# Attention, Fourier mixing and a two-layer MLP: a host layout without reversed copies, block 0 prepared inside the attention, and the blocks' loads spread

## The chip, the cores and the metric

One core of a Trainium2 chip. The time is the device time of one execution in microseconds (us). The engines are TensorE (PE; PEld is its weight load), VectorE (DVE), ScalarE (ACT), GpSimd (POOL) and SyncE (SP), which here only issues DMAs. A queue named SPq or POOLq is the sequencer that issues for that engine.

## The reference

```python
# q, k, v: (8, 8, 576, 64); per batch and head
out_d  = softmax(q_d k_d^T / 8) v_d     # q_d, k_d, v_d: means over 4 neighbours, 144 positions
out_lc = softmax(mask(q k^T / 8)) v     # mask: |i - j| < 4
x = repeat(out_d, 4) + out_lc           # as (8, 576, 512)
u = x + real(fft(fft(x, axis=1), axis=2))
un = (u - mean(u)) / sqrt(var(u) + 1e-6)
out = u + relu(un @ w_ch1) @ w_ch2      # 512 -> 2048 -> 512
```

## The kernel before

**Attention, some 330 us.** For each of 8 batches there are a pooled attention (`Pooled`, four pairs of heads), a local one (`Unit`, five spans of 128 positions, each with two windows of 64) and the Fourier part (`Mix`). `Unit.load` and `load_v` fetch `qkT` and `vaug` by SP; `sum_in` makes the pooled sums of four neighbours; `Pooled.sum_v` adds up four loads in `vsum` by accumulating DMAs of POOL. In the upper half of a batch the windows run backwards: `sum_in` writes reversed, and `Unit.copy_p` copies the transposed weights reversed and clears one column on POOL. `Mix` uses the symmetry in both axes: POOL adds a half of the columns to the other half, read reversed (`cross`), VectorE makes sum and difference (`fold`), ScalarE and POOL split into two parts (`split_high`, `split_low`), TensorE multiplies by waves (`sequence`, `mix`), and ScalarE copies the lower columns mirrored into the upper ones (`mirror`). Three results per batch go to DRAM: `ud` (pooled), `ul` (local) and `um` (mixed).

**Blocks, the rest.** 4608 tokens are 9 blocks of four tiles of 128. `Block.load` (693) brings a tile in three parts: part 0 copies `ul` in several pieces by SP (line 712), parts 1 and 2 add `um` (707) and `ud` (705) by accumulating DMAs of POOL. `stats`, `norm`, `turn` and `turn_high`/`turn_low` make the normed and transposed tile in two parts; `prepare` places them in the order. For each f of 16, `first` has 12 products (`hps`), `high` and `low` make the two parts of its relu, and `second` has 12 products into four sums (`acc`). `finish` adds and `store` writes out. Tiles and turned tiles are doubled: block n+1 uses the places of block n-1. The order is block 0 with f 0 to 4, block 1 with f 0 to 4, block 0 with f 5 to 15, then the rest of block 1 and blocks 2 to 8. The weights come as 64 quarters of 64-bit numbers; `Quarter` fetches each by SP and joins it on ACT, POOL and DVE (`size`, `clamp`, `join`, `high`, `low`). f 0 and 1 are decoded in the attention, the others behind it.

**The order.** Nothing is planned by cost. Every step is put in a list by `at(time, step)`; the times are numbers in the table `AT`, in units of which 20 are a batch (some 2 us each in the attention), and f takes 3.28 units. The steps are issued in the order of these numbers, each engine and queue runs its own in that order, and waits are put in where data or a place need it. `close_b` and `close_a` (838, 843) give places of the attention to the blocks: after `close_a` block 1 gets its tiles. Block 0's loads stand at units 120 to 160.5, its norms behind `close_b` (164.9), block 1's loads behind `close_a` (167.7). A later block's loads begin 6 units behind the start of the block ahead of it, its first norm at 12.

Of the kernel before, what the change touches and what calls it, by code (L numbers as in the profile page):

```python
# [22 lines left out]
    "pooled": (1.15, 0.05, -1.8, -2.74, -3.55),  # L23
    "mix": (18.82, 18.55, 17.92),
    "local_steps": (0, 1.66, 2.96, 4.76, 5.65, 7.95, 9.34),
    "pooled_steps": (0, 1.56, 3.05, 4.81, 5.63, 7.85, 9.33),
    "qk": (-12.1, 2.19),
    "sums": (-2.36, 0.44),
    "sum_v": (-12.96, -6.64, -4.76, 2.36),
    "load_v": (0.51,),  # L30
    "store_pooled": (0.1, 0.2),
    "crosses": ((1, 4.59), (2, 7.41), (0, 9.2)),
    "folds": ((3, 5.97), (1, 4.28), (2, 8.26), (0, 10.0)),
    "splits": (0.74, 0.9, 1.64),
    "z": (9.51, 12.03, 12.81, 15.82),
    "sequence": (12.92, 1.78, 0.82, 1.66),
    "mixed": (20.32, 2.6, 0.2, 0.9, 1.47, 2.03, 2.91),
    "store_local": (9.66,),
    "ffn": (3.75, 1.64),
    "decode": (49.49, 9.96, 8.98, 1.2, 1.74),  # L40
    "decode_steps": (-1.47, 0.24, 0.83, 2.1, 2.96),
    "first_norms": (0.57, 0.81, 2.43, 0.6),
    "second_norms": (0.03, 1.47, 0.8, 1.83),
    "add": (14.25, 2.77, 2.2),
# [6 lines left out]
TILES = 4  # L51
# [14 lines left out]
def kernel(  # L66
# [43 lines left out]
    um = [dram.tile([2, NSL * P, DM], F32, name=f"um{b}") for b in range(B)]  # L110
# [20 lines left out]
    unTs = {}  # L131
# [74 lines left out]
    maskb = p2.tile([P, W], BF16, name="maskb", bufs=1)  # L206
# [4 lines left out]
    nc.gpsimd.memset(odt[:, :, DM:], 0.0)  # L211
# [34 lines left out]
    class Pooled:  # L246
# [74 lines left out]
        def result(self, h0):  # L321
# [7 lines left out]
                out=odt[:GH, :, h0 * D : (h0 + 2) * D].rearrange("g t (h d) -> g t h d", h=2),  # L329
# [4 lines left out]
        def move(self):  # L334

            x = xab[self.b % 2]
            STORE.dma_start(out=odt[GH:GX, 0, :DM], in_=odt[W:GH, 1, :DM])
            STORE.dma_start(out=x[W:, NSL - 1, 0, :DM], in_=odt[:W, 1, :DM])

        def store(self):  # L340
            STORE.dma_start(out=ud[self.b].rearrange("(t g) c -> g t c", t=2), in_=odt[:GH, :, :DM])

        def plan(self):
            b = self.b
            stages = [self.scores, self.maxima, self.exps, self.transpose_p, self.copy_p, self.values, self.result]
            for r in range(4):
                at(pooled_at(b) + AT["sum_v"][r], self.sum_v, r)
# [10 lines left out]
    class Unit:  # L358
        def __init__(self, u):
            self.u, self.b, self.m = u, u // NPAIR, u % NPAIR  # L360
            self.s0 = SPANS[self.m]
            self.wins = [(st, st + W // 2 > HS) for st in STARTS[self.m]]

# [9 lines left out]
        def sum_in(self):  # L373

            if self.m == 0:
                sums[self.b] = pd.tile([P, 2, HP, G], F32, name="sums", bufs=1)
            g0 = self.s0 // 4
            lo = g0 if self.m == 0 else SPANS[self.m - 1] // 4 + P // 4
            hi = g0 + P // 4
            out = sums[self.b].rearrange("p i h g -> p (i h) g")  # L380
            x = self.qkT.rearrange("p i h (g r) -> p (i h) g r", r=4)
            for a, e in ((lo, min(hi, GH)), (max(lo, GH), hi)):
                if a < e:
                    to = out[:, :, a:e] if e <= GH else out[:, :, G + GH - 1 - a : G + GH - 1 - e : -1]
                    nc.vector.tensor_reduce(out=to, in_=x[:, :, a - g0 : e - g0], axis=AX.X, op=ALU.add)  # L385
# [51 lines left out]
        def copy_p(self):  # L437
            pT = self.pT = p2.tile([P, HP, 2, W], F32, name="pT", bufs=NUM_P)
            tpv = self.tp.rearrange("p (h n w) -> p h n w", h=HP, n=2)
            backs = [back for _, back in self.wins]  # L440
            if backs[0] == backs[1]:
                parts = [(slice(0, 2), backs[0])]
            else:
                parts = [(slice(n2, n2 + 1), back) for n2, back in enumerate(backs)]
            for r, back in parts:
                if back:

                    nc.gpsimd.memset(pT[:, :, r, 0:1], 0.0)
# [64 lines left out]
    class Mix:  # L513
# [8 lines left out]
        def cross(self, t):  # L522
            pq = self.pq[t] = psq.tile([P, 2, HD], F32, name="pq", bufs=3)
            xa, xb = (xab[self.b % 2][:, :, i] for i in range(2))
            for i, (u, v) in enumerate(((xa, xb), (xb, xa))):
                nc.gpsimd.tensor_tensor(out=pq[:, i], in0=u[:, t, 0:HD], in1=v[:, t, DM:HD:-1], op=ALU.add)


        def fold(self, t):
# [4 lines left out]
            else:  # L534
                a, b = odt[:, 0, 0:HD], odt[:, 0, DM:HD:-1]
# [511 lines left out]
```

## Time and profile before

| | us |
|---|---|
| median of 3 runs (lowest, highest) | 1204.2 (1194.73, 1205.47) |
| profiled execution, whole time | 1203.31 |
| its span, first to last instruction | 1201.5 |
| mean granted TensorE clock | 0.959 |
| TensorE, VectorE, ScalarE, GpSimd busy | 1108.2 (92%), 526.5 (44%), 366.0 (30%), 277.8 (23%) |

Each engine runs its own instructions in order, and busy time is the sum of their durations. "Idle before" is how long an engine stood before an instruction, and the name behind the arrow is what ended it. The granted clock is 1.00 at 2.4 GHz and 0.50 at 1.2 GHz. Only waits on the path to the end cost time.

### The profile page before, as it was taken

How to read it: one execution, taken by the hardware profiler on the slowest of the kernel's cores; microseconds unless marked ns; L12 is line 12 of the kernel's file. 1: busy time of each engine (PE TensorE's matmuls, PEld its weight loads, DVE VectorE, ACT ScalarE, POOL GpSimd, SP SyncE). 2: the span in 40 equal slices, each digit the busy share in tenths (PEclk: the TensorE clock that was granted, in tenths of full speed). 3: DMA queues.
4: the chain of work that ended last, by engine and by line, in shares of the span. 5: the costliest groups of instructions: out<-in, count | busy, mean ns of one | idle time of the engine just before them, and what ended most of it. 6: DMA issues, size and time to landing. Idle time of an engine off the chain costs nothing.

```text
span 1201.5 us, 20868 instructions
## 1 busy us (share of the span) xinstructions
PE 1108.2 (92%) x8304; PEld 927.0 (77%) x8304; DVE 526.5 (44%) x1218; ACT 366.0 (30%) x1102; POOL 277.8 (23%) x411
## 2 busy tenths in 40 slices
PE   4899889887868999999999999999999999899998
PEld 4788778776757888787788788788788788688887
DVE  3767777875678898222222221222222222122111
ACT  3667766784734444110110110111111111011010
POOL 2223432442484655203002001200200300200000
PEclk9788899997978999999999999999999999999999
DMA  9768667885684543605004103202301500500000
GB/s 293 196 182 261 207 176 217 287 238 140 160 229 121 143 124 97 140 1 127 14 1 109 31 1 96 44 1 75 66 1 50 91 1 36 106 1 1 35 1 35
DMA packets 59144, 124.12 MB, mean 103 GB/s; under 512 B 8024, under 2 KB 8152, under 8 KB 58792
## 3 DMA queue, kind: packets, MB, share of 16 engines
q1 hardware_dynamic: 45400, 93.25, 24.2%
q0 software_dynamic: 13648, 29.55, 14.2%
q8 instruction: 65, 1.06, 0.4%
q14 instruction: 31, 0.25, 0.1%
HBM read 89.89 MB, written 31.75 MB: 101 GB/s over the span
## 4 chain that ended last, share of the span: by engine, by line
PE 55%; DMA 8%; SPq 4%; DVE 3%; issue 1%; POOL 1%; ACT 0%; POOLq 0%; DVEq 0%; ACTq 0%
PE hps L767 26%; PE acc L785 9%; PE acc L786 9%; PE acc L787 9%; DMA ut<-ud 4%; DMA ut<-ul 3%; SPq L712 3%; DVE ut L791 1%; PE tpn L738 1%; PE mix L609 1%; POOL ut L707 1%; DVE st L719 1%; DVE hl L775 0%; DVE un L730 0%; ACT hh L771 0%
## 5 line engine op out<-in xcount | busy, mean ns | idle before, releaser
L767 PE MATMUL hps<-unT,w1h 128*128 128x512 f32 x1152 | 312.0, 393 | 0.0
L775 DVE SCALAR_TENSOR_TENSOR hl<-hps,hh 128x512 fp32r<-128x512 f32 x144 | 99.4, 690 | 477.0 <-ACT hh L771 476.9
L767 PEld LDWEIGHTS hps<-unT,w1h 128*128 128x128 f32 x1152 | 216.7, 189 | 45.9
L771 ACT ACTIVATE hh<-hps 128x512 fp32r<-128x512 f32 x144 | 85.9, 597 | 515.2 <-PE hps L767 515.2
L785 PE MATMUL acc<-w2h,hh 128*128 128x512 f32 x576 | 229.5, 398 | 0.0
L786 PE MATMUL acc<-w2l,hh 128*128 128x512 f32 x576 | 227.5, 395 | 0.0
L787 PE MATMUL acc<-w2h,hl 128*128 128x512 f32 x576 | 226.9, 394 | 0.0
L767 PE MATMUL hps<-unT,w1l 128*128 128x512 f32 x576 | 155.7, 392 | 0.0
L787 PEld LDWEIGHTS acc<-w2h,hl 128*128 128x128 f32 x576 | 109.9, 191 | 24.0
L785 PEld LDWEIGHTS acc<-w2h,hh 128*128 128x128 f32 x576 | 109.7, 190 | 22.8
L786 PEld LDWEIGHTS acc<-w2l,hh 128*128 128x128 f32 x576 | 109.7, 190 | 22.7
L767 PEld LDWEIGHTS hps<-unT,w1l 128*128 128x128 f32 x576 | 108.7, 189 | 23.6
L707 POOL DMA_DIRECT2D ut<-um x48 | 41.9, 1006 | 237.0 <-DMA ut<-ul 200.3
L723 POOL TENSOR_TENSOR rstd<-rstd,mhalf 128x1 f32<-128x1 f32 x36 | 20.2, 560 | 303.5 <-DVE rstd L722 303.5
L419 ACT ACTIVATE sb<-sc,mx 128x64 f32<-128x64 f32 x320 | 70.0, 330 | 1.3
L738 PE MATMUL tpn<-ident,un 128*128 128x128 f32 x144 | 25.6, 309 | 35.1 <-DVE un L730 35.1
L744 ACT CAST unT<-tpn 128x512 fp32r<-128x512 f32 x36 | 21.1, 586 | 118.1 <-PE tpn L738 118.1
L385 DVE TENSOR_REDUCE sums<-qkT 128x224 f32<-128x896 f32 (+4 forms) x48 | 44.0, 947 | 23.6 <-DMA qkT<-in_qk_dram 23.1
L738 PEld LDWEIGHTS tpn<-ident,un 128*128 128x128 f32 x144 | 19.5, 158 | 42.5 <-DVE un L730 38.5
L551 POOL TENSOR_TENSOR fl<-xeo,fh 128x512 fp32r<-128x512 f32 (+1 forms) x32 | 41.6, 1303 | 28.6 <-ACT fh L544 28.6
L571 PE MATMUL y<-seqm,fh 128*128 128x290 f32 (+1 forms) x256 | 44.3, 318 | 4.0 <-DVE x L479 3.1
L313 PE MATMUL avd<-vsum,ptd 72*72 72x65 f32 x512 | 42.2, 239 | 6.3 <-DMA vsum<-in_vg_dram 6.3
(92 smaller groups left out, 1393.7 us busy)
## 6 DMA issues: line engine op xcount, KB each, us to landing
qkT<-in_qk_dram SPq DMA_DIRECT2D x40, 512.0 KB
raw<-in_wq_dram SPq DMA_DIRECT2D x64, 256.0 KB
vaug<-in_vw_dram SPq DMA_DIRECT2D x40, 260.0 KB
out_dram<-ut SPq DMA_DIRECT2D x36, 256.0 KB
ul<-x SPq DMA_DIRECT2D x8, 1024.0 KB
um<-o SPq DMA_DIRECT2D x16, 512.0 KB
ut<-ud POOLq DMA_DIRECT2D x32, 256.0 KB, 6.4
vsum<-in_vg_dram POOLq DMA_DIRECT2D x24, 292.5 KB, 6.9
```

The source lines that it names most:

```text
L313: nc.tensor.matmul(av[:, t, hl, :], self.pts[h0][hl][:, kt, t * GH : (t + 1) * GH], self.vs[:, kt, h0 + hl, :], start=(kt == 0), stop=(kt ...
L385: nc.vector.tensor_reduce(out=to, in_=x[:, :, a - g0 : e - g0], axis=AX.X, op=ALU.add)
L419: nc.scalar.activation(out=self.sb[:, hp, h2], in_=sc[:, hp], func=AF.Exp, scale=0.125, bias=self.mx[:, h2, hp : hp + 1],)
L571: nc.tensor.matmul(y, l, r, start=(i == 0), stop=(i == len(mms) - 1))
L707: nc.gpsimd.dma_start(out=u[to : to + m], in_=um[b][j, k + j : k + j + m, :], accum_op=ALU.add)
L738: nc.tensor.transpose(tp[:, c * P : (c + 1) * P], self.un[i][:, c * P : (c + 1) * P], ident)
L767: nc.tensor.matmul(hps, a[:, c, :], unT[:, x, c, :], start=(i == 0), stop=(i == len(mms) - 1))
L771: nc.scalar.activation(out=hh, in_=self.hps[f], func=AF.Relu)
L775: nc.vector.scalar_tensor_tensor(out=hl, in0=self.hps[f], scalar=0.0, in1=self.hh[f].bitcast(F32), op0=ALU.max, op1=ALU.subtract)
L785: nc.tensor.matmul(acc, hh, w2h, start=start, stop=False)
L786: nc.tensor.matmul(acc, hh, w2l, start=False, stop=False)
L787: nc.tensor.matmul(acc, hl, w2h, start=False, stop=stop)
```

## The change

The host now lays the upper half of each batch backwards (`SPANS` holds the positions, the middle span joins a forward and a backward stretch, the last one runs over the end into padding), orders heads and mirrors columns (`HEAD_ORDER`, `COLUMNS`), and undoes it in the output and the weights. `sum_in` and `copy_p` have no reversed cases, `cross` and `fold` read forward, `mirror` is gone, and `um` holds 258 columns. A part 1 of `load` is two DMAs, one for each half of the columns. Block 0's part 0 is issued by POOL and not cut to `even_rows`. Block 0's loads, norms and turns move into the attention, and its `first` for f 0 and 1 ahead of the last sequence products. Three raw and three join places of the decoding, and `hh`, `hl`, move to a pool opened in `close_b`. The times in `AT` change, and the loads and norms of blocks 2 to 8 move.

```diff
-    "store_pooled": (0.1, 0.2),
+    "store_pooled": (0.1, 0.13),
-    "first_norms": (0.57, 0.81, 2.43, 0.6),
-    "second_norms": (0.03, 1.47, 0.8, 1.83),
-    "add": (14.25, 2.77, 2.2),
+    "first_norms": (89.93, -0.58, 91.0, 4.0),
+    "second_norms": (0.03, 1.47, 0.8, 1.93),
+    "add": (0, 2.77, 2.2),
+    "add0": (59.9, 3.96, 6.0),
+    "early": (3.97, 1.76),
+    "constants": (15.12, 26.0),
...
-    um = [dram.tile([2, NSL * P, DM], F32, name=f"um{b}") for b in range(B)]
+    um = [dram.tile([2, NSL * P, HN1], F32, name=f"um{b}") for b in range(B)]
...
         def copy_p(self):
             pT = self.pT = p2.tile([P, HP, 2, W], F32, name="pT", bufs=NUM_P)
-            for r, back in parts:
-                if back:
-                    nc.gpsimd.memset(pT[:, :, r, 0:1], 0.0)
-                    nc.scalar.copy(out=pT[:, :, r, 1:W], in_=tpv[:, :, r, W - 1 : 0 : -1])
-                else:
-                    nc.scalar.copy(out=pT[:, :, r], in_=tpv[:, :, r])
+            nc.scalar.copy(out=pT.rearrange("p h n w -> p (h n w)"), in_=self.tp)
...
-                nc.gpsimd.tensor_tensor(out=pq[:, i], in0=u[:, t, 0:HD], in1=v[:, t, DM:HD:-1], op=ALU.add)
+                nc.gpsimd.tensor_tensor(out=pq[:, i], in0=u[:, t, HD + 1 : DM + 1], in1=v[:, t, 0:HD], op=ALU.add)
...
-        def mirror(self, t):
-            n = outs[t]
-            for i in range(2):
-                nc.scalar.copy(out=self.o[:n, i, t, HD + 1 :], in_=self.o[:n, 1 - i, t, HD - 1 : 0 : -1])
...
                 elif part:
-                    nc.gpsimd.dma_start(out=u[to : to + m], in_=um[b][j, k + j : k + j + m, :], accum_op=ALU.add)
+                    for h, i, z in ((0, 1 - j, 1), (1, j, 0)):
+                        nc.gpsimd.dma_start(
+                            out=u[to : to + m, h * HD : h * HD + HD],
+                            in_=um[b][i, k + j : k + j + m, z : z + HD],
+                            accum_op=ALU.add,
+                        )
                 else:
-                    m = even_rows(min(m, STEP * n + STEP + 4 - k - j))
+                    m = min(m, STEP * n + STEP + 4 - k - j)
+                    if self.n:
+                        m = even_rows(m)
...
+                    eng = nc.sync if self.n else nc.gpsimd
...
-                at(t, self.first, f)
+                t_f = t_b + AT["early"][f] if self.n == 0 and f < CHUNKS[0] else t
+                at(t_f, self.first, f)
...
-            at(120 + AT["add"][0] * part + 4 * i, blocks[0].load, i, part)
+            start, step, step_part = AT["add0"]
+            at(start + step_part * part + step * i, blocks[0].load, i, part)
...
-                    at(starts[n] + 6 + 0.5 * i + 2 * part, blocks[n + 1].load, i, part)
-                v = starts[n] + 12 + i * (t - starts[n] - 18) / TILES
+                    at(starts[n] + 6 + i + 5 * part, blocks[n + 1].load, i, part)
+                v = starts[n] + 21 + i * (t - starts[n] - 27) / TILES
                 blocks[n + 1].prepare(i, v, v + 1)
```

## Rows read from the trace of the kernel before

**Rows 1.** The chain of waits, in order of time. Columns: start us, us, what. Two starts of a new f in block 8, and the four turns of a tile.

```profile
601.79 0.44 PE tpn L738 x4
...
1140.30 2.72 PE hps L767 x12
...
1145.73 2.72 PE hps L767 x12
```

**Rows 2.** Who waited for whom, of the whole span and then of 300 to 375 us. Columns: engine and line, what it waited for, us in total, times, longest us.

```profile
PE tpn L738 <- DVE un L730: 35.1, 11, 7.6
...
PE tpn L738 <- DVE un L730: 14.3, 4, 7.6
```

**Rows 3.** The chain of waits: the norm's statistics that follow the last load of a first tile, for block 3 and five blocks later for block 8.

```profile
569.38 0.70 DVE st L719
...
1038.60 0.71 DVE st L719
```

**Rows 4.** The timeline between 636 and 700 us, the change of one block. Columns: start us, us, engine, line, operation, tiles, count, idle before and what ended it.

```profile
642.23 2.48 DVE L791 TENSOR_TENSOR ut<-acc,ut 128x512 f32<-128x512 f32 x4
...
645.16 7.08 SPq L712 DMA_DIRECT2D ut<-ul  x20
...
656.67 0.85 POOL L707 DMA_DIRECT2D ut<-um  x1 [1.59 <-DMA ut<-ul]
...
657.21 3.00 POOL L705 DMA_DIRECT2D ut<-ud  x3
...
665.83 1.11 PE L738 MATMUL tpn<-ident,un 128*128 128x128 f32 x4 [2.76 <-DVE un L730]
```

**Rows 5.** TensorE between the attention's end and block 1, by the timeline; and a stretch of it with the busy time of each engine, the granted clock, the DMA engines' share and GB/s.

```profile
337.10 1.11 PE L738 MATMUL tpn<-ident,un 128*128 128x128 f32 x4 [7.64 <-DVE un L730]
...
365.69 1.12 PE L738 MATMUL tpn<-ident,un 128*128 128x128 f32 x4 [3.87 <-DVE un L730]
...
366.46 2.06 PE L767 MATMUL hps<-unT,w1h 128*128 128x512 f32 x4
...
335.00:340.00 5.00, 2.38 (x10) 2.01 (x11) 4.54 (x13) 1.00 (x3) 3.68 (x7) 0.50 1.02 329
```

**Rows 6.** Block 1's loads up to its first norm, on SP, POOL and DVE, by the timeline.

```profile
337.93 9.13 SPq L712 DMA_DIRECT2D ut<-ul  x21
...
345.67 1.91 POOL L707 DMA_DIRECT2D ut<-um  x2
...
350.00 3.46 POOL L707 DMA_DIRECT2D ut<-um  x4
...
353.88 4.58 POOL L705 DMA_DIRECT2D ut<-ud  x4
...
361.89 0.69 DVE L719 BATCH_NORM_STATS2 st<-ut 128x6 f32<-128x512 f32 x1 [4.28 <-issue]
```

**Rows 7.** Batch 7 in the attention: stretches of 5 us (busy time of each engine, clock, DMA share, GB/s), SP's issues and TensorE's waits by the timeline.

```profile
275.00:280.00 5.00, 0.67 (x4) 0.44 (x4) 1.00 (x4) 0.40 (x1) 2.57 (x4) 0.62 1.01 294
...
280.00:285.00 5.00, 1.91 (x9) 1.13 (x9) 3.83 (x11) 0.00 (x0) 0.00 (x0) 0.50 0.53 103
...
258.19 4.30 SPq L712 DMA_DIRECT2D ut<-ul  x3
...
264.99 5.75 SPq L712 DMA_DIRECT2D ut<-ul  x6
...
276.21 0.67 PE L294 MATMUL tp<-ident,sd 72*72 72x72 f32 x4 [2.44 <-DVE odt L328]
...
282.48 0.75 PE L268 MATMUL sp<-sums 64*72 64x144 f32 x2 [5.60 <-DVE yl L580]
```

**Rows 8.** Groups of instructions by line over the whole span. Columns: line, engine, operation, tiles, shapes, count | busy us, mean ns of one | idle before.

```profile
L628 ACT COPY o<-o 128x255 f32<-128x255 f32 (+1 forms) x48 | 17.1, 409 | 7.8 <-DVE o L622 7.6
...
L449 ACT COPY pT<-tpl 128x504 f32<-128x504 f32 (+1 forms) x24 | 12.3, 511 | 21.5 <-PE tpl L431 21.4
...
L451 ACT COPY pT<-tpl 128x512 f32<-128x512 f32 (+1 forms) x24 | 12.4, 517 | 7.5 <-PE tpl L431 7.3
...
L448 POOL MEMSET pT<- 128x8 f32 (+1 forms) x24 | 7.2, 390 | 6.4 <-PE av L460 6.4
...
L707 POOL DMA_DIRECT2D ut<-um x48 | 41.9, 1006 | 237.0 <-DMA ut<-ul 200.3 <-DVE hl L775 34.2 <-issue 2.4
...
L719 DVE BATCH_NORM_STATS2 st<-ut 128x6 f32<-128x512 f32 x36 | 24.7, 686 | 36.6 <-DMA ut<-ud 32.3 <-issue 4.3
...
L730 DVE TENSOR_SCALAR un<-ut,mv,rstd 128x512 f32<-128x512 f32 x36 | 21.0, 585 | 17.4 <-POOL rstd L723 17.3
...
L747 DVE TENSOR_TENSOR unT<-tpn,unT 128x512 fp32r<-128x512 f32 x36 | 24.5, 684 | 33.9 <-ACT unT L744 33.9
```

**Rows 9.** Who waited for whom between 60 and 330 us; and the stretch in which block 0's norms come to lie.

```profile
PE sc L394 <- ACT sb L419: 7.0, 11, 1.4
...
180.00:220.00 40.00, 34.46 (x619) 30.72 (x616) 32.06 (x93) 28.93 (x110) 15.11 (x25) 0.96 0.78 231
```

**Rows 10.** The DMA queue of POOL (packets, MB, share of 16 engines), its whole `um` issues (KB each, us to landing), and the stretch in which the weights are decoded.

```profile
q0 software_dynamic: 13648, 29.55, 14.2%
...
ut<-um POOLq DMA_DIRECT2D x24, 256.0 KB, 4.6
...
400.00:480.00 80.00, 80.00 (x354) 66.03 (x353) 71.48 (x135) 37.13 (x90) 49.15 (x75) 1.00 0.42 115
```

More of the change, by code (lines that the diff above doesn't have):

```diff
@@ L210 @@
     odt = pd.tile([GX, 2, DM + 2], F32, name="odt")
-    nc.gpsimd.memset(odt[:, :, DM:], 0.0)
+    nc.gpsimd.memset(odt[:, :, 0:1], 0.0)
     pbank = ExitStack()
@@ L376, in sum_in @@
                 sums[self.b] = pd.tile([P, 2, HP, G], F32, name="sums", bufs=1)
[L377 to L385, printed above, removed]
+            x = self.qkT.rearrange("p i h w -> p (i h) w")
+            to = sums[self.b].rearrange("p i h g -> p (i h) g")
+            for at0, g, n in SUMS[self.m]:
+                groups = x[:, :, at0 : at0 + 4 * n].rearrange("p h (g r) -> p h g r", r=4)
+                nc.vector.tensor_reduce(out=to[:, :, g : g + n], in_=groups, axis=AX.X, op=ALU.add)
         def scores(self):
@@ L465, in result @@
             full = slice(0, P)
-            xa, xb = (xab[self.b % 2][:, :, i, :DM] for i in range(2))
+            xa, xb = (xab[self.b % 2][:, :, i, 1 : DM + 1] for i in range(2))
             if self.m < 2:
@@ L486, in plan @@
             t = 4 * self.u
-            for fn, (first, step) in ((self.load, AT["qk"]), (self.sum_in, AT["sums"])):
+            for fn, (first, step) in ((self.load, AT["qk1" if self.b == 1 else "qk"]), (self.sum_in, AT["sums"])):
                 at(pooled_at(self.b) + first + step * self.m, fn)
@@ L613, in copy_odd @@
             if self.o is None:
-                self.o = pf.tile([P, 2, NSL, DM], F32, name="o", bufs=2)
-            nc.scalar.copy(out=self.o[: outs[t], 1, t, : HD + 1], in_=self.ps[t, 1][:, : HD + 1])
+                self.o = pf.tile([P, 2, NSL, HN1], F32, name="o", bufs=2)
+            nc.scalar.copy(out=self.o[: outs[t], 1, t], in_=self.ps[t, 1])
         def join(self, t):
             n = outs[t]
-            even = self.ps[t, 0][:, : HD + 1]
-            oa, ob = (self.o[:n, i, t, : HD + 1] for i in range(2))
+            oa, ob = (self.o[:n, i, t] for i in range(2))
             for o, op in ((oa, ALU.add), (ob, ALU.subtract)):
-                nc.vector.tensor_tensor(out=o, in0=even, in1=ob, op=op)
-        def mirror(self, t):
-            n = outs[t]
-            for i in range(2):
-                nc.scalar.copy(out=self.o[:n, i, t, HD + 1 :], in_=self.o[:n, 1 - i, t, HD - 1 : 0 : -1])
+                nc.vector.tensor_tensor(out=o, in0=self.ps[t, 0], in1=ob, op=op)
         def store(self):
@@ L663, in plan @@
                 at(u + low, self.sequence_low, T)
-            first, step, even, copy, join, mirror, store = AT["mixed"]
+            first, step, even, copy, join, store = AT["mixed"]
             for i in range(NSL):
@@ L691, in __init__, with load @@
             self.hps, self.hh, self.hl = {}, {}, {}
-        def load(self, i, part):
-            u, tt = uts[self.n % 2][i], self.n * TILES + i
+        def load(self, t, part):
+            u, tt = uts[self.n % 2][t], self.n * TILES + t
             g, e = tt * P, (tt + 1) * P
@@ L835 @@
     t_e = last + AT["sequence"][0] + 3 * AT["sequence"][1] + 0.1
-    t_d = last + AT["mixed"][0] + 2 * AT["mixed"][1] + AT["mixed"][6] + 0.1
+    t_d = last + AT["mixed"][0] + 2 * AT["mixed"][1] + AT["mixed"][5] + 0.1
     def close_b():
         p1.close()
-        pools["early"] = pool("early")
-        unTs[0] = pools["early"].tile([P, 2, NCC, TILES * P], F32R, name="unT0")
+        pools["turn"] = pool("turn")
+        decode_places(pools["turn"], 3, 3)
     def close_a():
@@ L930, in _constants @@
     j = np.arange(64)
-    mask = np.where(np.abs(i[:, None] - j[None, :]) < 4, 0.0, -8e9).astype(np.float32)
+    near = np.abs(i[:, None] - j[None, :]) < 4
+    own = (i[:, None] == 0) == (j[None, :] == 0)
+    mask = np.where(np.stack([near, near & own], axis=1), 0.0, -8e9).astype(np.float32)
     k1 = np.arange(S // 2 + 2)
@@ L975 @@
 STEP, WINDOW, NPAIR, SEQ, HEADS, DIM = 57, 64, 5, 576, 8, 64
-FWD = [STEP * m for m in range(NPAIR)]
-BWD = [SEQ - WINDOW - st for st in FWD]
-STARTS = [(FWD[0], FWD[1]), (FWD[2], FWD[3]), (FWD[4], BWD[4]), (BWD[2], BWD[3]), (BWD[0], BWD[1])]
-SPANS = [0, 112, 228, 340, 448]
+HEAD_ORDER = [7, 6, 5, 4, 0, 1, 2, 3]
+STARTS = [(0, STEP), (2, 2 + STEP), (0, WINDOW), (5, 5 + STEP), (3, 3 + STEP)]
+SPANS = [
+    [*range(0, 128)],
+    [*range(112, 240)],
+    [*range(228, 292), *range(348, 284, -1)],
+    [*range(467, 339, -1)],
+    [*range(579, 451, -1)],
+]
+COLUMNS = [*range(HEADS * DIM - 1, HEADS * DIM // 2 - 1, -1), *range(HEADS * DIM // 2)]
+SUMS = [[(0, 0, 32)], [(16, 32, 28)], [(12, 60, 12), (65, 129, 15)], [(0, 99, 30)], [(4, 72, 27)]]
 _OUTS = [((8, 576, 512), "float32")]
@@ L1019, in _tokens @@
     t = np.arange(SEQ)
-    return rows[:, np.where(t < SEQ // 2, t, SEQ + SEQ // 2 - 1 - t)]
+    rows = rows[:, np.where(t < SEQ // 2, t, SEQ + SEQ // 2 - 1 - t)]
+    return rows[:, :, np.argsort(COLUMNS)]
 def kernel(**inputs):
```

98 lines of the change are left out of this document (47 added, 51 removed).

## The prediction

> **What bounds the kernel now.** I read the busy line and the 40 slices first: TensorE is busy 92% of the span and the last two thirds are nearly all its own work. The chain that ended last shows its rhythm: a new f, that is 12 products of `first` and 12 of `second`, starts every 1145.73 - 1140.30 = 5.43 us, and a tile's four turns take 0.44 us [rows 1]. A block of 16 f and four tiles should take 16 x 5.43 + 4 x 0.44 = 88.6 us. The view of waits says where it takes longer: TensorE waits for `un` 11 times, 35.1 us in all; four of these, 14.3 us, lie between 300 and 375 us, so seven, 20.8 us, lie at the changes from one block to the next [rows 2]. The norms that end such waits, five blocks apart, stand at 569.38 and 1038.60 us: 93.8 us per block, 5.2 us over the 88.6 [rows 3]. 2.97 us of it are the wait; the rest is mostly half clock behind it.
>
> One change of block shows why [rows 4]. The tiles of block n+1 take the place of those of block n-1. `finish` writes these at 642.23, the stores follow, SP then issues 20 pieces of `ul` (7.08 us), POOL's last `um` goes at 656.67, the first `ud` at 657.21, and the turn runs at 665.83 after TensorE stood 2.76 us. TensorE had reached that turn at 663.1, since the program puts it 13.8 units behind the block's start.
>
> The second place is the end of the attention [rows 5]. After its last product, at 329.5 us, TensorE stands 7.64 us until block 0's first turn, runs on at half clock (0.50 between 335 and 340), stands again at 365.69 for block 1's first turn, and takes 2.06 us for four products that take some 1.1 us later. Block 1's chain is long [rows 6]: its 21 pieces of `ul` leave SP from 337.93 to 347.1, its six `um` leave POOL from 345.67 to 353.5, `ud` starts at 353.88, and the norm at 361.89.
>
> The third place is batch 7 in the attention [rows 7]. SP is held 4.30 and 5.75 us by block 0's `ul` pieces, between the loads that batch 7 waits for; TensorE then stands 2.44 and 5.60 us, the clock falls to 0.62 and 0.50, and the DMA engines are full (1.01).
>
> **The change, part by part.** All against the profiled execution, 1203.3 us (span 1201.5 and 1.8 around it); the three timed runs have a median of 1204.2, so 0.9 is added at the end.
>
> *Block changes.* Three things move: `ul`, `um` and `ud` of a block lie 5 units apart in place of 2, the first norm's turn stands at 22.8 units behind the start in place of 13.8, and each `um` part is two issues. Loads keep their order on SP and POOL, and nothing but the powers of the norms stands behind them on POOL, later in the order. Nine units are 2.74 f, and counted out in the order of TensorE five more groups of 12 products stand ahead of the turn (12 in place of 7), 5 x 2.72 = 13.6 us. The chain grows by what the second `um` of the last tile costs: one issue, 0.85 us [rows 4], up to 1.0 [rows 8], and the smaller rows. A queue-0 packet takes 14.2% of 16 x 1201.5 us over 13648, 0.20 us, for 2 KB [rows 10]; at 1 KB between 0.10 and 0.20, so 512 rows of a block add nothing to 512 x 0.2 / 16 = 6.4 us. I take 2.5. The waits are 2.97 us in the mean; for one half as long again 4.5 + 0.85 + 2.5 = 7.9 us are needed, and 13.6 are there. All seven waits go. The loss per change is 2.97 plus half clock, by the period 5.2; where the clock didn't fall it is the wait alone. 7 x 2.97 = 20.8 to 7 x 5.2 = 36. I take -30; ends 0 (the chain fills its new room) and -36.
>
> By the Trainium skill, "DMA: Bandwidth & Descriptors", section "Anatomy of one DMA — SWDGE (gpsimd) path", a transfer from GpSimd costs about 2.0 us beside its bytes, so that two halves cost 2 us more than one whole. If that were paid one after the other, block 1's six more issues would make its chain some 12 us longer, and the forecast 7.5 us later. The rows speak against paying it in series: issues leave POOL one per 0.9 us [rows 6] while one lands in 4.6 us [rows 10], so several are under way at once.
>
> *Batch 7.* Block 0's loads move to units 59.9 to 84, some 123 to 173 us, and `ul` from SP to POOL; SP's 19 pieces are gone (counted out with `even_rows`), nine of them the two holds of 4.30 and 5.75 us. The stalls are 8.0 us, and the clock behind them costs about 3 us more. Not all is SP's: the DMA engines were full too, from block 0's bytes and batch 7's own. Ends 0 and -12; I take -8. What is late next there is the vaug load, 1 to 2 us.
>
> *ScalarE.* The mirror copies go: 48, 17.1 us; 48 copies of pT (24.7 us) become 40 of 0.52: -4 us [rows 8]. TensorE waits on ScalarE's exponentials for 7.0 us in 11 waits [rows 9], which bounds what can show from above; ends 0 and -7, I take -4. POOL loses 24 clears, 7.2 us.
>
> *Block 0's norms* (stats 0.69, `un` 0.59, low part 0.68 [rows 8], and two small ones: some 2.3 us x 4 = 9.2 us of VectorE) move to units 88 to 105, about 180 to 215 us. VectorE is busy 32.1 of 40 us there, TensorE 34.5 [rows 9]: 8 us of room in gaps that the pipeline doesn't choose. Nothing to +9.2; I take +4. The 16 turns, 1.8 us of TensorE, are in it.
>
> *Block 0's loads on POOL.* 12 `ul`, 10 `um`, 4 `ud` = 26 issues where POOL had 9: 17 more at 1.0 us, less the clears. Queued behind them stand crosses, splits and the next vsum part of batches 2 and 3. The `um` is a batch old and 6 units stand between the parts, so none should wait. 0 to +10; I take +2.
>
> *Host order, forward reads.* Same shapes and element counts; `sums` keeps six reductions per batch, `fold` and `cross` their sizes. The `um` stores lose half their bytes. Bounds: a reversed copy of 504 elements takes 511 ns and a forward one of 512 takes 517 [rows 8], so nothing is won by direction; the stores' bytes bound it at 0 to -2 us, and I take 0.
>
> *End of the attention.* first1, first0 now fill the 7.64 us, and first2 no longer stands behind block 1's turn in the order (177.96 against 178.04). But the sequence products still wait for the last split, which waits for the last unit's result, and behind first2 TensorE waits for block 1. That chain isn't moved: SP's order there is the same, and six more `um` issues stand on POOL ahead of `ud`: 6 x 0.9 = 5.4 us, less 1 because POOL's powers for block 0 are gone: block 1's turn comes 4.5 us later, near 370. What is saved is first2, 2.7 us at full clock, some 3 with a part at half. Net +1.5. Ends: all waits of [rows 2] there and the half clock given back, 14.3 + 5 = -19, and +8 if the smaller rows come on top.
>
> *Decoding.* VectorE is busy 71.5 of 80 us between 400 and 480 [rows 10] and delivers weights just ahead of their use. Block 1 starts later, not earlier, against it, so this cover holds; if the start came 19 us earlier, the 8.5 us of room would not do, and TensorE could wait some 10 us for weights.
>
> Sum: -30 - 8 - 4 + 4 + 2 + 1.5 = -34.5: 1203.3 - 34.5 = 1168.8; plus 0.9, rounded down: 1169 us.
>
> **The rivals.**
> A. *The end of the attention is given back too.* For it: TensorE's idle and half clock there are 19 us, and first0, first1 fill the first hole. Against it: block 1's loads. If block 1's chain were not the bound, -17 in place of +1.5: 1151 us, or up to 10 later where the weights are late.
> B. *The chain fills its new room.* If the doubled `um` makes the loads 14 us longer, only part of the change-of-block loss returns, say 5 us: 1169 + 25 = 1194. Against it: the last tile alone is late in [rows 4]; the others' `um` leave while POOL would idle.
> C. *Slower: POOL held by block 0's accumulating loads.* Each of 14 (`um`, `ud`) must wait until the part before has landed, 4.6 us [rows 10]; if POOL stands for it in order and crosses and splits stand behind, up to 14 x 4.6 = 64 us show in batches 3 and 4: 1169 - 2 + 64 = 1231. It decides from 36.5 / 14 = 2.6 us per issue on. Against it: 6 units, 12 us, between the parts.
> D. *It doesn't do what it says*: the loads still meet full DMA engines earlier on, and the attention loses what batch 7 gains and 20 us more: 1197.
>
> **How the numbers follow.** Forecast 0.60, A 0.20, B 0.10, C 0.05, D 0.05. This kernel can tell 1% (12 us) from no change. Faster by over 1% (below 1192): the forecast, A, and a third of B, 0.84. Within 1%: the rest of B and D, 0.11. Slower: C, 0.05. The likeliest's own range is 1157 to 1182: the parts' bounds of 6 to 8 us, not all to one side. For 8 in 10 it reaches into A and toward B: 1147 to 1187.
>
> **What would show it.** Right: seven turns at block changes without a wait, blocks 89 us apart, clock 1.00 from 420 us on; no wait for qkT in batch 7; block 1's first turn still waiting, near 362 (370 less the attention's 6 to 8 us). Wrong: turns that wait as before (B); TensorE without a hole between the attention's end and block 1 (A); POOL standing at block 0's `um` between 135 and 175 us (C).

## The result, and the profile after

The median went from 1202.72 to 1166.3 us (four runs each, 1164.54 to 1168.33 after); the ratio is 0.9708, 95% interval 0.9658 to 0.9758. The forecast was 1169. The profiled execution took 1165.94 us with a span of 1164.2, 37.3 less than before. The sum was nearly hit, its terms less so. Three stages by the timelines, cut at the attention's last group of `av` and at block 1's first turn:

| us of the profiled executions | before | after | difference | forecast |
|---|---|---|---|---|
| start to the last group of `av` | 328.76 | 315.52 | -13.2 | -6 |
| from there to block 1's first turn | 36.93 | 37.22 | +0.3 | +4.5 |
| from that turn to the end | 835.8 | 811.5 | -24.3 | -33 |

(The forecast of the last stage is the -30 of the block changes and the 3 of `first` 2, which left this stage; that of the middle one is the turn's delay alone.)

The page of after: the busy line, the granted clock in 40 slices, POOL's queue, and the bytes.

```profile
PE 1094.0 (94%) x8304; PEld 912.7 (78%) x8304; DVE 529.9 (46%) x1218; ACT 352.7 (30%) x1046; POOL 323.4 (28%) x447
...
PEclk7799988899988999999999999999999999999999
...
q0 software_dynamic: 19536, 30.62, 15.7%
...
HBM read 89.92 MB, written 27.05 MB: 100 GB/s over the span
```

From the fourteenth slice (378 us) on the clock is high throughout. POOL's packets grew from 13648 to 19536 and their share by 1.5 points only [rows 10].

Who waited for whom in after, whole span. It answers to [rows 2] and [rows 9]:

```profile
PE tpn L725 <- DVE un L717: 10.9, 4, 8.1
...
PE sc L393 <- ACT sb L418: 3.6, 5, 1.5
```

Eleven waits of 35.1 us became four of 10.9; they lie at 196, 353, 365 and 370 us, none at a change of block behind these. One such change, by the timeline, against [rows 4]:

```profile
622.31 2.48 DVE L778 TENSOR_TENSOR ut<-acc,ut 128x512 f32<-128x512 f32 x4
...
625.25 6.93 SPq L699 DMA_DIRECT2D ut<-ul  x20
...
629.20 1.78 POOL L687 DMA_DIRECT2D ut<-um  x2 [33.37 <-DMA ut<-ul]
...
636.27 1.74 POOL L687 DMA_DIRECT2D ut<-um  x2 [0.89 <-DMA ut<-ul]
...
637.37 3.34 POOL L684 DMA_DIRECT2D ut<-ud  x3
...
656.59 0.60 PE L725 MATMUL tpn<-ident,un 128*128 128x128 f32 x4
```

The turn stands 34.3 us behind `finish` (23.6 before) and waits for nothing. The chain up to the first `ud` takes 15.1 us where it took 15.0, although `um` is eight issues in place of four: the doubled issues fit in between the landings of `ul`.

The end of the attention in after, by the timeline, answers to [rows 5, 6]:

```profile
328.62 1.57 PE L558 MATMUL y<-seqm,fh 128*128 128x290 f32 x5 [4.50 <-ACT fh L531]
...
330.66 5.22 POOL L687 DMA_DIRECT2D ut<-um  x6
...
342.07 5.59 POOL L684 DMA_DIRECT2D ut<-ud  x5
...
343.01 0.73 PE L754 MATMUL hps<-unT,w1l 128*128 128x512 f32 x2 [2.28 <-POOL w1l L200]
...
349.42 0.69 DVE L706 BATCH_NORM_STATS2 st<-ut 128x6 f32<-128x512 f32 x1 [4.48 <-DMA raw<-in_wq_dram]
...
352.74 1.11 PE L725 MATMUL tpn<-ident,un 128*128 128x128 f32 x4 [8.06 <-DVE un L717]
```

Block 0's 7.64 us hole is filled, but 4.50 and 2.28 us of new ones stand behind it, and block 1's wait rose from 3.87 to 8.06. Together 14.8 us of idle stand there where the four waits of [rows 2] had 14.3: TensorE is early and block 1's chain is not.

Two stretches of batches 3 and 4, and the blocks (busy time of PE, PEld, DVE, ACT, POOL; clock; DMA share; GB/s):

```profile
145.00:150.00 5.00, 4.58 (x43) 4.44 (x41) 4.51 (x8) 3.55 (x15) 0.00 (x0) 1.00 1.08 300
150.00:155.00 5.00, 2.87 (x71) 2.79 (x72) 1.21 (x2) 0.83 (x4) 3.93 (x7) 0.62 0.96 263
...
175.00:215.00 40.00, 32.42 (x521) 28.24 (x511) 35.45 (x95) 25.16 (x88) 13.51 (x20) 0.91 0.69 195
...
370.00:700.00 330.00, 329.57 (x1459) 269.41 (x1460) 145.65 (x277) 75.09 (x159) 100.18 (x143) 1.00 0.31 74
700.00:1150.00 450.00, 450.00 (x1987) 367.21 (x1987) 100.92 (x181) 57.43 (x97) 62.45 (x78) 1.00 0.19 40
```

From 370 to 1150 us TensorE is idle for 0.4 us in all, at a clock of 1.00, as forecast. Yet the blocks are longer than the 88.6 us of the forecast. The chain of after: the first turns of two blocks that stand two apart, a start of f in an odd block, and two in block 8:

```profile
837.03 0.44 PE tpn L725 x4
...
1017.30 0.44 PE tpn L725 x4
...
1045.98 2.72 PE hps L754 x12
...
1090.51 2.81 PE hps L754 x12
...
1096.08 2.81 PE hps L754 x12
```

Two blocks take 180.27 us, not 177.2. In block 8 the 12 products of `first` take 2.81 us and an f 5.57, where [rows 1] had 2.72 and 5.43; in odd blocks they still take 2.72 (1045.98). The even blocks read the turned tile unT0, which the change allocates elsewhere. `second`, which reads no turned tile, also takes 5.57 - 2.81 = 2.76 us there in place of 2.71; why isn't shown.

To place the attention's gain, the steps between the ends of consecutive batches (last reciprocal of a batch's last unit, from the timelines of VectorE), us:

| step to batch | 1 | 2 | 3 | 4 | 5 | 6 | 7 |
|---|---|---|---|---|---|---|---|
| before | 45.8 | 40.0 | 40.9 | 38.7 | 37.1 | 46.6 | 31.8 |
| after | 37.1 | 37.6 | 43.2 | 45.1 | 36.9 | 34.3 | 30.6 |
| b1_layout | 40.8 | 36.0 | 37.7 | 37.0 | 35.4 | 42.9 | 31.9 |
| b5_sp | 38.1 | 37.7 | 56.5 | 44.9 | 36.8 | 34.3 | 30.7 |
| e2_pool_late | 36.6 | 38.1 | 39.9 | 34.9 | 36.4 | 36.6 | 34.7 |

The hole of [rows 7] lies in step 6. Each row is one execution. A step moves by some 2 to 4 us between executions that differ elsewhere, so only the larger differences are read.

### The profile page after: what moved, and what is told of

The parts are those of the page before. It is cut to its first block, busy times and chain, and to the rows that moved or that the text cites. A ratio compares the mean times of both kernels' runs of the same rounds, so it can differ in the third digit from the quotient of the medians.

```text
span 1164.2 us, 20852 instructions
## 1 busy us (share of the span) xinstructions
PE 1094.0 (94%) x8304; PEld 912.7 (78%) x8304; DVE 529.9 (46%) x1218; ACT 352.7 (30%) x1046; POOL 323.4 (28%) x447
## 3 DMA queue, kind: packets, MB, share of 16 engines
q1 hardware_dynamic: 44706, 87.50, 23.6%
q0 software_dynamic: 19536, 30.62, 15.7%
## 4 chain that ended last, share of the span: by engine, by line
PE 68%; DVE 2%; POOL 1%; DMA 1%; issue 1%; SPq 0%; ACT 0%; DVEq 0%; ACTq 0%; POOLq 0%
PE hps L754 33%; PE acc L773 11%; PE acc L772 11%; PE acc L774 11%; PE tpn L725 1%; DMA raw<-in_wq_dram 1%; POOL ut L687 1%; DVE wt L182 0%; SPq L699 0%; POOL pq L513 0%; DVE ut L778 0%; DVE wt L179 0%; DVE st L706 0%; DVE un L717 0%; POOL fl L538 0%
## 5 line engine op out<-in xcount | busy, mean ns | idle before, releaser
L754 PE MATMUL hps<-unT,w1h 128*128 128x512 f32 x1152 | 315.5, 396 | 0.0
L754 PEld LDWEIGHTS hps<-unT,w1h 128*128 128x128 f32 x1152 | 214.1, 188 | 47.1
L772 PE MATMUL acc<-w2h,hh 128*128 128x512 f32 x576 | 225.7, 392 | 0.0
L687 POOL DMA_DIRECT2D ut<-um x96 | 85.2, 1533 | 208.1 <-DMA ut<-ul 174.5
L734 DVE TENSOR_TENSOR unT<-tpn,unT 128x512 fp32r<-128x512 f32 x36 | 24.8, 689 | 57.5 <-ACT unT L731 57.5
L558 PE MATMUL y<-seqm,fh 128*128 128x290 f32 (+1 forms) x256 | 44.9, 320 | 6.4 <-ACT fh L531 4.5
L384 DVE TENSOR_REDUCE sums<-qkT 128x256 f32<-128x1024 f32 (+5 forms) x48 | 43.4, 946 | 12.8 <-DMA qkT<-in_qk_dram 12.0
L684 POOL DMA_DIRECT2D ut<-ud x40 | 47.0, 1958 | 2.4 <-DMA ut<-um 2.4
L538 POOL TENSOR_TENSOR fl<-xeo,fh 128x512 fp32r<-128x512 f32 (+1 forms) x32 | 41.5, 1301 | 22.1 <-ACT fh L531 13.4
L318 PEld LDWEIGHTS avd<-vsum,ptd 72*72 72x72 f32 x512 | 39.8, 153 | 8.9 <-issue 8.0
```

Of the source, the lines that this page charges most:

```text
L318: nc.tensor.matmul(av[:, t, hl, :], self.pts[h0][hl][:, kt, t * GH : (t + 1) * GH], self.vs[:, kt, h0 + hl, :], start=(kt == 0), stop=(kt ...
L384: nc.vector.tensor_reduce(out=to[:, :, g : g + n], in_=groups, axis=AX.X, op=ALU.add)
L558: nc.tensor.matmul(y, l, r, start=(i == 0), stop=(i == len(mms) - 1))
L684: nc.gpsimd.dma_start(out=u[to : to + m], in_=groups, accum_op=ALU.add)
L687: nc.gpsimd.dma_start(out=u[to : to + m, h * HD : h * HD + HD], in_=um[b][i, k + j : k + j + m, z : z + HD], accum_op=ALU.add,)
L754: nc.tensor.matmul(hps, a[:, c, :], unT[:, x, c, :], start=(i == 0), stop=(i == len(mms) - 1))
```

## The experiments

### The spacing of the blocks alone (a1_spacing)

```diff
 # before
-                    at(starts[n] + 6 + 0.5 * i + 2 * part, blocks[n + 1].load, i, part)
-                v = starts[n] + 12 + i * (t - starts[n] - 18) / TILES
+                    at(starts[n] + 6 + i + 5 * part, blocks[n + 1].load, i, part)
+                v = starts[n] + 21 + i * (t - starts[n] - 27) / TILES
```

> The kernel before with the blocks' loads and norms spread as in the change (5 units between the parts, the first norm 21 units behind the start), and nothing else. If the waits at the block changes are a matter of the turn's place in TensorE's order, all seven go with the half clock behind them: 28 to 34 us less than before, some 1169 to 1175, no wait of a turn behind 420 us. If the loads fill whatever room they get, the waits shrink to half at most: 1187 or more.

1175.39 us, ratio 0.9782 [0.9742, 0.9822], against 1200.86. The waits of a1_spacing:

```profile
PE tpn L738 <- DVE un L730: 15.0, 4, 7.6
```

Only the four at the attention's end are left. From block 1's first turn (364.84) to the end (1172.5) it takes 807.7 us, 28.1 less than before. The term of -30 stands. Rival B needs the doubled `um`, which this kernel doesn't have: it falls by after itself, whose turns don't wait at a change, and by b1_layout below.

### The place of unT0 (a2_pad, a3_pad_all, c2_unT0_32)

```diff
 # after; a2_pad (a3_pad_all: the first pad ahead of the weights of f 0 and 1 instead)
+    res.tile([P, 8], F32, name="pad0")
     unTs = {0: res.tile([P, 2, NCC, TILES * P], F32R, name="unT0")}
+    res.tile([P, 8], F32, name="pad1")
 # c2_unT0_32: 104 in place of the first 8, 24 in place of the second
```

> The changed kernel with 32 bytes of padding ahead of block 0's turned tile and 32 behind it, so that this tile begins at 32 modulo 64 bytes in place of 0, as the other turned tile and the weights from f 2 on do. In the changed kernel's trace an f takes 5.57 us in blocks 0, 2, 4, 6, 8 and 5.44 in the odd ones. If the place of the tile against the weights is the cause, 75 f become 0.13 us shorter: 10 us less, 1156, and even blocks at 5.44. If the cause is another one (the two halves of the um loads, the relu's places), nothing moves: 1166, even blocks at 5.57.

> As the run with the padding around block 0's turned tile, but the padding stands ahead of the weights of f 0 and 1, so that these too begin at 32 modulo 64. If the place against each other counts, f 0 and 1 also drop from 5.57 to 5.44 in all nine blocks: 18 x 0.13 = 2.3 us more, 1154. If not, 1156 to 1166 as that run gives.

> The kernel after with 416 bytes ahead of unT0 and 96 behind it: unT0 goes from byte 44160 (128 mod 512) to 44576 (32 mod 512, as unT1 and as unT0 in the kernel before), and everything behind keeps its remainder mod 512. Theory P512 (the even blocks' products are slower because unT0 and the weights lie at different remainders mod 512): 12 products of first take 2.72 us in even blocks too, except f 0 and 1 (2.81); an even block's f takes 5.44 in place of 5.57 us, some 75 x 0.13 = 10 us are won, and the time is 1156 to 1158. Rival P64 (only the remainder mod 64 counts): 2.76 as with 32 bytes of shift, time 1161 to 1167. Rival Q (the products are not what the time follows, since a shift of 32 bytes gave half of them back and no time): 2.72, but the time stays at 1164 to 1167 and some other wait has grown.

a2_pad took 1167.23 us (0.9720 [0.9682, 0.9758]), a3_pad_all 1164.05 (0.9684 [0.9641, 0.9727]), c2_unT0_32 1160.51 (0.9659 [0.9603, 0.9714]). The intervals overlap that of after, so the products themselves are the evidence. Block 8 in the chain of a2_pad, then of c2_unT0_32 with the first turns of two blocks that stand two apart:

```profile
1135.36 2.76 PE hps L756 x12
...
1140.89 2.76 PE hps L756 x12
```

```profile
833.00 0.44 PE tpn L727 x4
...
1011.92 0.44 PE tpn L727 x4
1012.35 2.77 PE hps L756 x12
...
1062.85 2.81 PE hps L756 x12
...
1095.93 2.72 PE hps L756 x12
...
1101.37 2.72 PE hps L756 x12
```

With unT0 at byte 44160 (128 mod 512) the twelve products take 2.81 us, at 44192 (160) 2.76, at 44576 (32, as unT1 has) 2.72. Two blocks take 178.92 us in c2_unT0_32, and from block 1's first turn to the end 804.8 in place of 811.5: the place cost 6.7 us, not the 10 that were expected. It isn't unT0's address alone: with it at remainder 32 the products of f 0 in block 8 still take 2.81 us (1062.85) and those of f 4 and later 2.72, and f 0 differs by its weights, which the kernel allocates in another pool. In a3_pad_all, which moves the weights of f 0 and 1 too, f 0 takes 2.76 us in block 8 (2.78 in after), so the expected fall to 2.72 didn't come. Which remainders count, and against what, stays open.

c2_unT0_32 also shows what a block costs without any loss: 178.92 / 2 = 89.46 us, 0.9 more than the 88.6 of the prediction, which took every f at 5.43 us. The products of f 0 (2.81) and those behind a turn (2.77, at 1012.35) take longer than 2.72.

### The host's layout with the new table (b1_layout)

```diff
 # after, unT0 as in c2_unT0_32
-    "first_norms": (89.93, -0.58, 91.0, 4.0),
+    "first_norms": (0.57, 0.81, 2.43, 0.6),
-            at(start + step_part * part + step * i, blocks[0].load, i, part)
+            at(120 + 14.25 * part + 4 * i, blocks[0].load, i, part)
-                t_f = t_b + AT["early"][f] if self.n == 0 and f < CHUNKS[0] else t
+                t_f = t
-                    eng = nc.sync if self.n else nc.gpsimd
-                    eng.dma_start(...)
+                    nc.sync.dma_start(...)
 ...  # spacing of the blocks and even_rows as in before, norms of block 0 from t_b; the rest of AT as in after
```

> The kernel after with the places in the order put back to those of before: spacing of the blocks' loads and norms, block 0's loads (SP, even rows), norms and first products; unT0 at a remainder of 32 mod 512. What is left of the change is the host's layout: no reversed copies, no mirror, um half as wide and added by two DMAs per part. Theory (layout nearly neutral in the attention, doubled um lengthens the block's chain): attention ends 0 to 6 us earlier than before's 329.5, the seven waits at block changes are 0.9 to 3.4 us longer than before's 2.97, time 1200.9 - 4 + (6 to 24) = 1203 to 1221. Rival L (the layout is where the attention's 13 us come from): attention ends 10 us or more earlier, near 317; time near 1195. Rival B for the block changes (halves cost no more than a whole): waits of 3 us as before, time 1191 to 1197.

1187.24 us, ratio 0.9882 [0.9810, 0.9955], against 1204.26. The last group of `av` starts at 312.23 us: 16.5 earlier than before, and 3.3 earlier than in after. The waits of b1_layout, over the whole span and from 370 us on:

```profile
PE tpn L725 <- DVE un L717: 35.0, 11, 7.7
...
PE tpn L725 <- DVE un L717: 20.4, 7, 4.1
```

Rival L holds: the layout, with the attention's new places in the table, gives all of the attention's gain. Block 0's part inside the attention adds nothing to it: in these two executions steps 3 and 4 lose 13.6 us (37.7 and 37.0 against 43.2 and 45.1), step 6 wins 8.6, the rest is -1.7, and 3.3 us are lost in all. The 3.3 are not clear of noise, since the four executions of b1_layout lie 9.3 us apart; nor is all of step 3, which takes 41.8 and 41.0 us in d1_old_places and d2_mirror below. Step 4 (37.3 and 37.0 there) and step 6 (44.0 and 44.1) are. The second number is also an answer: seven waits of 20.4 us, as the 20.8 before, with twice as many `um` issues. The halves cost the block changes nothing.

### Why the layout pays (d1_old_places, d2_mirror, d3_bytes)

```diff
 # b1_layout; d1_old_places: the table AT of before, wherever it has the entry
 # d2_mirror
+        def mirror(self, t):
+            n = outs[t]
+            for i in range(2):
+                nc.scalar.copy(out=self.o[:n, i, t, 1:HD], in_=self.o[:n, i, t, 1:HD])
...
+                at(u + join + 0.56, self.mirror, i)
 # d3_bytes, in store
+                u = um2[self.b][i]
+                STORE.dma_start(out=u[: 2 * P].rearrange("(t p) c -> p t c", p=P), in_=self.o[:, i, : NSL - 1])
```

> b1_layout with the table of places AT put back to the values of before wherever before has them (batch 1's own places of qk and sum_v go too). In b1_layout the attention's last product ends at 312.9 us, in before at 329.5. Theory (the host's layout gives it: fewer ScalarE copies, no reversed reads, half the um bytes): the attention ends at 312 to 317 us and the time is 1186 to 1192. Rival (the new places of the table give it, the layout nearly nothing, as was forecast): it ends at 325 to 330 us, the time is 1199 to 1204.

> b1_layout with the 48 mirror copies put back on ScalarE as copies of the same 255 columns in their own place (17.1 us in before); they change nothing in the data. Theory (ScalarE's time is a large part of the layout's gain): the attention ends at 319 to 328 us in place of 312.9, the time is 1194 to 1203. Rival (ScalarE has room; the bytes or the other edits give it): it ends at 312 to 315 us, the time is 1186 to 1190.

> b1_layout with a second store of the first 256 rows of each half of um into DRAM that nothing reads: the mixed part's stores move nearly as many bytes as before, by two more SP issues per batch. Theory (bytes of the stores held the loads of qkT): the attention ends at 319 to 328 us in place of 312.9, with DVE's waits for qkT up from 8.4 toward 15.2 us. Rival (they are hidden): it ends at 312 to 315 us, the time is 1186 to 1190.

| | us | ratio | last group of `av` |
|---|---|---|---|
| b1_layout | 1187.24 | 0.9882 [0.9810, 0.9955] | 312.23 |
| d1_old_places | 1195.42 | 0.9932 [0.9902, 0.9961] | 317.98 |
| d2_mirror | 1192.07 | 0.9892 [0.9828, 0.9955] | 321.55 |
| d3_bytes | 1201.9 | 0.9999 [0.9966, 1.0033] | 323.94 |

Only d3_bytes is apart from b1_layout, by 14 us by the ratios and 11.7 by the last group of `av`; with it the layout's gain in time is gone, though the attention still ends 4.8 us earlier than before. VectorE's wait for `qkT` in the first 331 us, of b1_layout and then of d3_bytes (before had 23.1 us in 13):

```profile
DVE sums L386 <- DMA qkT<-in_qk_dram: 16.1, 13, 5.2
```

```profile
DVE sums L387 <- DMA qkT<-in_qk_dram: 23.5, 14, 5.3
```

So the halved stores of `um` are the one part that is shown to count: with 4.2 MB more written the waits for `qkT` are 7 us longer again, and the clock of the attention falls from 0.91 to 0.89. d3_bytes also adds two issues per batch on SP; one takes 0.40 us in the median, 0.8 us a batch, so the bytes look the likelier cause, but the two aren't told apart. The attention of d1 and d2 ends 5.8 and 9.3 us later than that of b1_layout, by the ratios they are 6 and 1 us slower, and neither time separates. The three differences add to more than the 16.5 us, so they can't be read as shares: how much the new places and the mirror copies are worth stays open. That the layout gains without the new places too, d1 shows: 0.9932 lies below 1 with its whole interval.

### SP or POOL for block 0's pieces (a4_b0_early, b5_sp)

```diff
 # before: a4_b0_early
-            at(120 + AT["add"][0] * part + 4 * i, blocks[0].load, i, part)
+            at(59.9 + 6.0 * part + 3.96 * i, blocks[0].load, i, part)
 # after: b5_sp
-                    eng = nc.sync if self.n else nc.gpsimd
-                    eng.dma_start(...)
+                    nc.sync.dma_start(...)
```

> The kernel before with block 0's loads alone moved to units 59.9 to 84, still by SP and in whole rows, its norms where they were. If batch 7's hole comes from SP being held by these pieces and from their bytes, TensorE stands no more between 270 and 285 us, and 6 to 12 us go: 1191 to 1197. If the hole only moves to batches 3 and 4 with the loads, the time stays: 1199 to 1206.

> The kernel after with block 0's ul pieces issued by SP in place of POOL, at the same places in the order. Theory SP (SP held by these pieces, between the loads that a batch waits for, made the holes of batch 7 before and of batch 3 where they had only been moved): batch 3 shows a wait for qkT or sums of some 5 to 10 us near 170 to 190 us, the attention ends 5 to 10 us later than 316.1, time 1171 to 1176. Rival DMA (full DMA engines made the holes, and the halved um stores are what cured them): no such wait, attention ends within 2 us of 316.1, time 1164 to 1168.

a4_b0_early took 1205.8 us, 1.0042 [1.0005, 1.0080]; b5_sp 1177.7, 0.9793 [0.9740, 0.9847]. (The pieces of a4_b0_early are still cut by `even_rows`, other than its expectation says.) TensorE in a4_b0_early, and in b5_sp with three stretches of 5 us (columns as above):

```profile
171.34 1.50 PE L268 MATMUL sp<-sums 64*72 64x144 f32 x8 [10.51 <-DVE sums L385]
```

```profile
166.92 2.02 PE L273 MATMUL sp<-sums 64*72 64x144 f32 x8 [6.47 <-DVE yl L567]
...
145.00:150.00 5.00, 5.00 (x46) 4.78 (x44) 3.93 (x6) 3.12 (x13) 0.00 (x0) 1.00 1.05 224
...
165.00:170.00 5.00, 2.73 (x14) 1.67 (x15) 4.33 (x13) 0.29 (x1) 0.11 (x1) 0.50 0.41 58
170.00:175.00 5.00, 4.48 (x26) 4.22 (x26) 2.34 (x7) 3.02 (x14) 2.19 (x3) 0.50 0.32 36
```

The last loads of the batch on SP and VectorE's wait for `qkT` from 125 to 190 us, of after and then of b5_sp:

```profile
143.23 1.39 SPq L374 DMA_DIRECT2D vaug<-in_vw_dram  x2
...
DVE sums L384 <- DMA qkT<-in_qk_dram: 3.9, 2, 3.6
```

```profile
153.40 0.96 SPq L374 DMA_DIRECT2D vaug<-in_vw_dram  x2
...
DVE sums L384 <- DMA qkT<-in_qk_dram: 13.9, 3, 6.6
```

By SP the hole only moves with the loads, into step 3 (56.5 us in b5_sp, 54.2 in a4_b0_early), with the half clock behind it: the loads leave SP 10 us later, and VectorE waits 10 us longer for them. The attention ends 14.9 us later than in after, more than the 5 to 10 expected. By POOL, the one line that differs between b5_sp and after, step 3 takes 43.2, although the DMA engines are just as full (1.08 at 145 us, 1.05 in b5_sp). So the theory of SP's hold stands: full engines alone don't make the hole. What they cost in after, where the clock also falls to 0.62 behind 150 us, no run separates.

### Block 1's `ud` earlier (b3_ud_first)

```diff
 # after: um of tiles 0 and 1, ud 0, um 2, ud 1, um 3, ud 2, ud 3
-            at(t_a + AT["add"][1] + 0.1 * i + AT["add"][2] * part, blocks[1].load, i, part)
+            at(t_a + AT["add"][1] + (0.1 if part == 0 else 0.9) * i + AT["add"][2] * min(part, 1) + 1.0 * (part == 2), blocks[1].load, i, part)
```

> The kernel after with block 1's accumulating loads in another order: um of tiles 0 and 1, ud of 0, um of 2, ud of 1, um of 3, ud of 2 and 3, in place of all um and then all ud, so that the first ud stands ahead of about 5 issues of 0.9 us on POOL. Theory (block 1's chain through POOL sets the end of the attention's hole): the first turn of block 1 runs 3 to 5 us earlier than at 352.74, the wait ahead of it is 3 to 5 us in place of 8.06, time 1161 to 1163. Rival (the landing of ul, not POOL's issues, is what comes last, or the later turns lose what the first wins): first turn within 1 us of 352.7, or waits at the following turns that grow by as much; time 1165 to 1167.

1171.71 us, 0.9742 [0.9689, 0.9795]: not better than after. Tile 0 of block 1 in b3_ud_first:

```profile
348.24 0.69 DVE L706 BATCH_NORM_STATS2 st<-ut 128x6 f32<-128x512 f32 x1 [0.98 <-issue]
...
348.52 4.12 POOL L687 DMA_DIRECT2D ut<-um  x2
...
353.09 1.06 POOL L710 TENSOR_TENSOR rstd<-rstd,mhalf 128x1 f32<-128x1 f32 x1
...
354.19 0.55 DVE L717 TENSOR_SCALAR un<-ut,mv,rstd 128x512 f32<-128x512 f32 x1 [2.04 <-POOL rstd L710]
...
354.79 1.12 PE L725 MATMUL tpn<-ident,un 128*128 128x128 f32 x4 [7.80 <-DVE un L717]
```

The tile is complete earlier, its statistics standing 30.7 us behind the last group of `av` (33.9 in after), but the power of its norm stands on POOL behind the `um` and `ud` issues that my order put ahead of it, and waits until 353.09. The expectation failed in the time; POOL's one queue still sets the turn, through another instruction. From that turn to the end it takes 816.1 us in place of 811.5, and the second turn comes 11.0 us behind the first in place of 6.3, so what follows loses more than the rival allowed. The first turn itself stands 37.3 us behind the last group of `av`, as in after (37.2).

### A version beyond both (e2_pool_late)

```diff
 # b1_layout
+                    if self.n:
+                        m = even_rows(m)
+                    eng = nc.sync if self.n else nc.gpsimd
+                    eng.dma_start(...)
 ...  # and the spacing of the blocks as in after
```

> The kernel after with unT0 at a remainder of 32 mod 512 and block 0's loads, norms and first products put back to their places of before (loads at units 120 to 160, norms and first products behind the attention), but with its ul on POOL as in after; spacing of the other blocks as in after. Against b1_layout it changes the spacing and ul's queue. Theory (block 0 inside the attention costs batches 3 and 4 what it saves in batch 7, since 5.5 and 8.1 us longer steps stand against 8.6; and SP's hold is what batch 7 lost): the step to batch 7 falls from 42.9 us in b1_layout to 34 to 38, the attention ends at 305 to 309 us, block 1's first turn runs near 345 to 348, the time is 1154 to 1158 against 1160.5 of c2. Rival (any place pays the same: the bytes of block 0 cost some 8 us wherever they lie): attention ends at 312 to 314, time 1160 to 1163.

1155.57 us, 0.9611 [0.9564, 0.9658]: some 11 us below after's 0.9708, whose interval it only touches; beside c2_unT0_32 not apart by the times and 6.4 us by the spans. Its waits and block 1's turn:

```profile
PE tpn L727 <- DVE un L719: 15.2, 4, 7.7
```

```profile
346.97 1.12 PE L727 MATMUL tpn<-ident,un 128*128 128x128 f32 x4 [6.32 <-DVE un L719]
```

Step 6 takes 36.6 us with block 0's loads back in their late place but on POOL (42.9 by SP); step 7 takes 34.7, some 3 us more than in the other rows, so a part comes back. The hole of [rows 7] needed another queue, not an earlier time.

## Why the prediction was right, and where its terms were not

**Right in the sum by errors that cancel**: 7.2 us too little for the attention, 4.2 too much delay at its end, 8.7 too much for the blocks.

*Block changes, -30.* Right: -28.1 alone (a1_spacing), -31.0 with `first` 2 gone and unT0 well placed (c2_unT0_32, 33 forecast). The waits went for the reason given: the turn came 10.7 us later behind `finish` and the wait of 2.76 was gone, 13.4 of the 13.6 us counted out. The price of 5.2 us per change was too high. Against the 89.46 us that a block takes without a loss, the 93.8 of [rows 3] leave 4.4, seven times 30.7 and not 36, so the range's far end was 5 us out. The 0.85 + 2.5 us for the doubled `um` didn't show: 20.4 us of waits with it, 20.8 without. The Trainium skill's 2.0 us per transfer ("DMA: Bandwidth & Descriptors", section "Anatomy of one DMA — SWDGE (gpsimd) path") is not paid in series here; a half of 128 KB lands in 4.7 us, a whole one took 4.6 [rows 10].

*What I left out: the place of unT0*, +6.7. The prediction has no term for it. Of the operand's address the Trainium skill ("SBUF — State Buffer", section "Operand start alignment") asks only a multiple of the element size, and says that its runs there timed nothing; these do, 2.72 to 2.81 us.

*Host order, 0, and ScalarE, -4: the mis-sized terms.* Together -16.5 (b1_layout, with the table's new places, which had no term). The step that failed is "the stores' bytes bound it at 0 to -2 us": 4.2 MB of stores put back, with two issues a batch, made the attention 11.7 us longer (d3_bytes). I priced the bytes as transfer time; what they cost shows in the loads of `qkT` that come late ahead of `sums`, 7 us, and in the lower clock.

*Batch 7, -8, block 0's norms and loads, +4 and +2.* Step 6 gave -8.6 against b1_layout; steps 3 and 4 cost 13.6, not 6 (9 to 10 against d1_old_places and d2_mirror). Forecast -2 in all, measured +3.3, which isn't clear of noise. Step 4 holds the norms, at a clock of 0.91 and 35.45 of 40 us of VectorE; norms and loads weren't run apart. The cause I named first, SP's hold, was right, but the cure is the queue and not the earlier place. The two can't be split within after, since an early place by SP (b5_sp) costs 13 us in step 3.

*End of the attention, turn +4.5.* +0.3. The twelve `um` issues do take 11.4 us (330.66 to 342.07) where six took 7.8 (345.67 to 353.46), but they start 1.8 us earlier against the attention's end, and `ud` to turn shrank by 1.1. That block 1's wait would stay was right; rival A did not come.

*Rivals.* B fell (after, b1_layout). C: its 64 us would stand in steps 3 and 4, which lost 13.6 in all. POOL doesn't stand before an `um` of block 0. D came in part at most: the loads do meet full engines in batches 3 and 4, but that these cost the 13.6 us isn't shown. (The chances add to 0.83 and 0.12 where the prediction has 0.84 and 0.11.)

*Signs.* Seven turns without a wait, the clock of 1.00 and no wait for `qkT` in batch 7 came. Blocks stand 90.1 us apart in place of 89, and block 1's first turn came at 352.7 us, not near 362, since the attention gave more and its end lost less.

## What to carry to other kernels

Bytes that stand beside a stage's loads can be worth what waits for those loads, not only their own transfer time. For a load that holds a queue, try another queue before another time. After moving a tile to another pool, compare the mean time of the products that read it.

## What was not expected of the hardware

Products of `first` with the same shapes took 2.81, 2.76 and 2.72 us per twelve in three kernels that differ in the padding around the tile they read (44160, 44192, 44576), at a granted clock of 1.00: some 3%, in five of nine blocks. The weights' place counts too, since f 0 took 2.81 us with the tile at 44576; the rule is not known.
